# Two-layer spectral and squared-ReLU kernel: x loaded in pairs ahead of the constants, first-stage matrices scaled on POOL and ACT, mirrored filter rows placed by transfers, a new order table

## The chip, the cores and the metric

The kernel runs on one core of one Trainium2 chip. A core has five engines that run side by side and meet at semaphores: TensorE (PE, matmuls; its weight loads are shown as PEld), VectorE (DVE), ScalarE (ACT), GpSimd (POOL) and SyncE (SP, which here only issues transfers). Sixteen DMA engines move the data; SP, ACT and POOL issue to them. The metric is device time in microseconds (us), the median of several runs. The profile is of one further execution, and its times are counted from the first instruction.

## The reference

`x` is 2048 tokens by 448 features in bf16. Two layers are applied, each of a spectral part A and a dense part B, with the same weights in both layers:

```
def _A_ref(x, w_r, w_i):
    X = rfft2(x.astype(float32))
    X = X * (w_r + 1j * w_i)
    return irfft2(X, s=(S, D)).astype(bfloat16)

def _B_ref(x, w1, b1, w2, b2):
    h = einsum("bsd,df->bsf", x, w1) + b1
    h = relu(h) ** 2
    return einsum("bsf,fd->bsd", h, w2) + b2

x = x + _A_ref(_layernorm(x), A_w_r, A_w_i)
x = x + _B_ref(_layernorm(x), B_w1, B_b1, B_w2, B_b2)
x = x + _A_ref(_layernorm(x), A_w_r, A_w_i)
x = x + _B_ref(_layernorm(x), B_w1, B_b1, B_w2, B_b2)
```

The filter `w_r`, `w_i` has 2048 rows of 225 columns. The dense part goes from 448 to 1792 features and back.

## The kernel before

The tokens lie as 128 partitions by 16 tiles; a tile `t` is `[128, 448]`. Both Fourier transforms are written as matmuls with constant matrices. The work of layer 0 up to its dense part runs in these stages:

- **A1**, for each tile: mean and variance (`ln_stats`, on DVE with `bn_stats` and `bn_aggr`, or for tiles 1, 4 and 6 on ACT in two passes over the tile), the square root on ACT, the reciprocal `rstd` on DVE, and `m`, minus twice the mean (`minus`, L805). `first_A` then scales the 128x256 matrix `FA_sb` by `rstd` into a buffer `Fs` (L673) and lets PE multiply the tile by it: four products of 256 columns and one with `m`. The result is moved from the accumulators (`ps`) to `XA`. There are four buffers `Fs`, used in turn: the scaling for tile t waits until PE is done with tile t-4.
- **TD** and **B**, for each of eight frequency pairs: products with `TD_sb` (out to `U`) and with `G_sb` (out to `EF`); `U` and `EF` are parts of the buffer `arena`.
- **W**, the product with the filter, all on DVE: chains of `tensor_tensor` (L688) on `EF` and the filter rows in `Wt`. For a frequency pair, four rows are read: two as they lie in DRAM and two in mirrored order. The first chain, W0.0, reads the first frequency pair of `Wt`; the last, W0.7, ends the stage.
- **Bi**, **TI**, **AI**: the way back, products with `H_sb`, `HS_sb`, `TI_sb`, `FI_sb`; PE can do a part of Bi only when W has written its input. The stage ends in `x_sb`. The dense part follows, with `W1_sb` and `W2_sb`, then the same again for layer 1.

The mirrored filter rows come in three steps. POOL issues two gathers (L704) that read the rows of `w_i` and of `w_r` backwards into `Wm`, which lies in the buffer `yT`. When they have landed, POOL copies 14 pieces of 128x224 from there to `Wt` (L744 through the helper line L662). The other constants are loaded by plain transfers that SP issues, all of them after tile 4 of x has landed (`x4`, L747).

What sets the order: every operation is recorded once, and a scheduler (`schedule`) sorts the recorded units by the numbers in the table `ORDER`; a letter behind a number gives the engine (`p` POOL, `a` ACT, `d` DVE). While it walks the sorted list it keeps a model of the times of each engine. By this model it picks one of the eight accumulator banks for each result, and puts warming matmuls (on a matrix of ones, L1307) before a PE unit where the model says PE would wait. Each engine then runs its own instructions strictly in this order. The waits between engines are derived from which bytes are read and written.

Of the kernel before, what the change touches and what calls it, by code (L numbers as in the profile page):

```python
# [1384 lines left out]
```

## Time and profile before

| | us |
|---|---|
| median of 3 runs | 269.33 |
| lowest and highest run | 268.26 and 269.40 |
| span of the profiled execution, first to last instruction | 267.8 |

The time of the profiled execution as a whole is not given apart; the three runs lie 0.5 to 1.6 us above its span. In the page, "busy" is the time in which an engine had an instruction running. The rows of a timeline give the start and the length of a group of like instructions, then engine, line, operation, output and inputs, their shape and number, and in brackets how long the engine sat idle before them and what ended that. The rows that the prediction reads are quoted there.

### The profile page before, as it was taken

Reading aid. Unit: us, or ns where it says so; the run is one execution under the profiler, and the core shown is the slowest. Engines: PE = TensorE matmul, PEld = TensorE weight load, DVE = VectorE, ACT = ScalarE, POOL = GpSimd, SP = SyncE. Lnnn points to the kernel's source line nnn. Section 1 sums busy time; section 2 is a strip of 40 time slices with the busy share of each in tenths; the row PEclk is TensorE's granted clock in tenths of the full one; section 3 lists DMA queues with packets and bytes.
Section 4 is the critical chain, followed back from the end, with each engine's and each line's share of the span. In section 5 each row is a group of like instructions: output and inputs, shape, how many; then the busy total and the mean of one; then the engine's idle time right before and its main releaser. Section 6 shows DMA issues by size and latency. Waiting matters only on the chain. (4 is left out here: it accounts for less than half of the span.)

```text
span 267.8 us, 5840 instructions
## 1 busy us (share of the span) xinstructions
PE 259.3 (97%) x2194; PEld 158.9 (59%) x2194; DVE 212.7 (79%) x652; ACT 171.3 (64%) x391; POOL 14.4 (5%) x42
## 2 busy tenths in 40 slices
PE   6899999899999999999999999989999999999996
PEld 1477665798544544555559774779654554454554
DVE  5866999899996964999999899899998963463722
ACT  4688994979429755985128896889735753678000
POOL 0577000000000000000000000000000000000000
PEclk9999999999999999999999999999999999999999
DMA  6999370020420222300000000011232026200211
GB/s 222 305 376 354 74 228 17 0 42 10 54 52 2 39 43 44 68 0 0 2 0 4 2 2 0 2 23 22 39 73 42 0 42 111 89 2 0 70 39 47
DMA packets 27312, 17.03 MB, mean 64 GB/s; under 512 B 20210, under 2 KB 25810, under 8 KB 27156
## 3 DMA queue, kind: packets, MB, share of 16 engines
q1 hardware_dynamic: 26692, 14.82, 21.7%
q10 hardware_dynamic: 432, 1.03, 1.1%
q0 software_dynamic: 160, 0.81, 0.8%
q8 instruction: 17, 0.28, 0.5%
q14 instruction: 11, 0.09, 0.1%
HBM read 11.15 MB, written 1.84 MB: 48 GB/s over the span
## 5 line engine op out<-in xcount | busy, mean ns | idle before, releaser
L636 PE MATMUL ps<-yT,W_sb 64*128 64x512 bf16 (+1 forms) x770 | 90.3, 346 | 0.0
L636 PE MATMUL ps<-W_sb,arena 128*128 128x448 bf16 (+2 forms) x490 | 87.5, 336 | 0.0
L636 PEld LDWEIGHTS ps<-yT,W_sb 64*128 64x128 bf16 (+1 forms) x770 | 51.5, 95 | 36.0 <-issue 1.5
L636 PEld LDWEIGHTS ps<-W_sb,arena 128*128 128x128 bf16 x490 | 46.3, 98 | 36.3 <-DVE arena L688 0.8
L655 ACT ACTIVATE arena<-ps,b1col 128x512 bf16<-128x512 f32 x84 | 51.9, 691 | 14.2 <-PE ps L636 14.0
L688 DVE TENSOR_TENSOR arena<-arena 128x512 bf16<-128x512 bf16 (+1 forms) x140 | 45.7, 367 | 18.0 <-ACT arena L655 17.6
L1109 ACT ACTIVATE VT<-x_sb 128x448 bf16<-128x448 bf16 x32 | 18.4, 577 | 13.4 <-DVE x_sb L1085 13.3
L661 ACT ACTIVATE arena<-ps 128x448 bf16<-128x448 f32 (+1 forms) x44 | 25.1, 693 | 2.4 <-PE ps L636 2.2
L1205 DVE SCALAR_TENSOR_TENSOR x_sb<-ps,arena 128x448 bf16<-128x448 f32 (+2 forms) x27 | 15.2, 570 | 14.1 <-PE ps L636 13.7
L655 ACT ACTIVATE mv<-mv,epst 128x1 f32<-128x1 f32 (+1 forms) x46 | 12.6, 294 | 17.2 <-DVE mv L794 12.1
L655 ACT ACTIVATE arena<-ps 128x256 bf16<-128x256 f32 x56 | 17.8, 392 | 4.0 <-PE ps L636 3.7
L661 ACT ACTIVATE XA<-ps 128x512 bf16<-128x512 f32 x29 | 15.6, 592 | 3.2 <-PE ps L636 3.2
L661 ACT ACTIVATE VT<-ps 128x512 bf16<-128x512 f32 (+1 forms) x26 | 13.0, 567 | 7.0 <-PE ps L636 6.9
L636 PE MATMUL ps<-yT,VT 64*128 64x512 bf16 x42 | 15.8, 376 | 0.0
L636 PE MATMUL ps<-HS_sb,arena 128*128 128x512 bf16 x64 | 14.9, 380 | 0.1
L636 PE MATMUL ps<-arena,G_sb 128*128 128x448 bf16 (+1 forms) x76 | 14.4, 333 | 0.5 <-ACT arena L661 0.4
L672 ACT ACTIVATE arena<-x_sb,rstd 128x448 bf16<-128x448 bf16 x11 | 7.2, 666 | 10.5 <-DVE rstd L1124 6.0
L636 PE MATMUL ps<-TD_sb,XA 112*64 112x112 bf16 (+2 forms) x312 | 13.2, 224 | 0.0
L636 PE MATMUL ps<-Fs,xin 128*128 128x256 bf16 x64 | 10.0, 290 | 3.0 <-DVE mv L784 2.9
L636 PEld LDWEIGHTS ps<-TD_sb,XA 112*64 112x64 bf16 (+2 forms) x312 | 12.1, 108 | 1.1 <-issue 0.6
L688 DVE TENSOR_TENSOR tmp<-arena,Wt 128x896 bf16<-128x896 bf16 (+1 forms) x14 | 11.4, 852 | 1.7 <-ACT arena L661 1.5
L1135 DVE SCALAR_TENSOR_TENSOR arena<-x_sb,mv,b2row 128x448 bf16<-128x448 bf16 x16 | 10.7, 679 | 0.1
(76 smaller groups left out, 300.9 us busy)
## 6 DMA issues: line engine op xcount, KB each, us to landing
out_dram<-x_sb SPq DMA_DIRECT2D x15, 112.0 KB, 1.7
W_sb<-in_B_w_dram SPq DMA_DIRECT2D x1, 1568.0 KB, 16.1
W_sb<-in_B_w_dram SPq DMA_DIRECT2D x1, 1344.0 KB, 6.7
HS_sb<-c_HS SPq DMA_DIRECT2D x1, 1024.0 KB, 11.2
G_sb<-c_G SPq DMA_DIRECT2D x1, 960.0 KB
...
Wt<-in_A_w_i_dram SPq DMA_DIRECT2D x1, 392.0 KB, 4.7
```

Of the source, the lines that this page charges most:

```text
L636: return sch.add("pe", lambda e: e.matmul(_res(o), lhsT, rhs, start=start, stop=stop, skip_group_check=skip), [lhsT, rhs], [o], cost=cost, ...
L655: sch.add("act", lambda e: e.activation(o, _res(i), func, **kw), rd, [o], cost=c)
L661: op = sch.add(engs[0], lambda e: e.activation(o, _res(i), ACT.Copy) if h[0].eng == "act" else e.tensor_copy(o, _res(i)), [i], [o], cost=c ...
L672: op = sch.add(engs[0], lambda e: e.activation(o, i, ACT.Copy, scale=s) if h[0].eng == "act" else e.tensor_scalar(o, i, s, 1.0, op0=ALU.mu ...
L688: sch.add(eng, lambda e: e.tensor_tensor(o, _res(a), b, op), [a, b], [o], cost=_free(o) / rate + 69.0)
L1109: sch.add("act", lambda e, i=i, o=o, x=x: e.activation(o, x, ACT.Square, accum_out=mv[:, i, 4:5]), [x], [o, mv[:, i, 4:5]], cost=560.0)
L1135: small(lambda e, o=o, x=x, m=m: e.scalar_tensor_tensor(out=o, in0=x, scalar=m, in1=b2row[:], op0=ALU.add, op1=ALU.add), [x, m, b2row[:]], ...
L1205: small(lambda e: e.scalar_tensor_tensor(out=o, in0=_res(i), scalar=r[0] if r else 1.0, in1=xb[:, t, d0:d1], op0=ALU.mult, op1=ALU.add), [ ...
```

## The change

It has six parts, all in the first stages of layer 0 and in the order table.

1. **x in pairs.** The 16 tiles came in seven transfers of one or four tiles; they now come as tile 0, tile 1 and then pairs. SP issues tile 0 and six pairs, ahead of all constants; ACT issues tile 1, `FA_sb` (before: SP's third transfer) and tiles 4 and 5. The constants now wait for tile 7 and no longer for tile 4.
2. **Scaling on POOL and ACT.** The scaled matrix of each tile is written to the tile's own place in `x_sb`, which is free at that time, and not to one of four buffers. 15 of the 16 scalings are on POOL and one on ACT; before, 10 were on POOL and 6 on DVE. The clearing of `x_sb`'s spare columns moves behind A1.
3. **Mirrored rows by transfers.** The 14 copies on POOL are replaced by two transfers from `Wm` to `Wt` that SP issues; they run backwards over seven rows of 224. The two gathers are moved to the front of POOL's work and wait for tile 0 only.
4. **Unbroken dummies.** The warming matmuls are no longer put in by the scheduler's model; a table `WARM` gives 15 of them in one run before the first product of A1.
5. **Banks in the table.** The bank of each result now stands in `ORDER` behind a colon; the model of times in `schedule` is gone. The walk through the sorted list adds the waits for a bank's last readers as before.
6. **A new `ORDER`.** Units of A1, TD, B, W, Bi, TI and AI of layer 0 and of the first part of its dense stage stand in another order. From the middle of that dense part on, the order is the old one with numbers lower by ten.

```diff
-    "dve.warm": "1", "dve.epst": "4", "sp.xin": "0 12 15 18", "act.xin": "11 14 17", "sp.FA_sb": "13",
+    "dve.warm": "2", "dve.epst": "3", "sp.xin": "4 8 11 12 13 14 15", "act.xin": "6 9", "act.FA_sb": "7",
...
-    "A1.0": "6 7 24 26 9p 28d 64 99a", "A1.1": "23 25 30 32 39 27d 70p 71 111a", "A1.2": "20 21 29 34 22p 67p 68 78a",
+    "A1.0": "5 26 29 30 32d 31p 53:0 60a", "A1.1": "27 34 36 37 41 28p 42p 66:1 88a", "A1.2": "33 39 46 47 40p 52p 68:2 135d",
...
+WARM = {53: ((7, 512), (7, 512), (7, 512), (7, 512), (7, 512), (7, 512), (7, 512), (7, 512), (7, 512), (7, 512), (7,
+    512), (7, 512), (7, 512), (7, 256), (7, 128))}
...
     def schedule(self):
...
+        for n, u in enumerate(self.ranked()):
+            for b, w in WARM.get(n, ()):
+                d = _Op("pe", self.warm_fn(b, w), False, 0.0, 0.0)
+                take(b, d)
...
-        for n, (a, b, e) in enumerate(((0, 1, "sp"), (1, 2, "act"), (2, 3, "sp"), (4, 8, "act"), (3, 4, "sp"), (8, 12, "act"),
-                                       (12, 16, "sp"))):
+        for n, (a, b, e) in enumerate(((0, 1, "sp"), (1, 2, "act"), (2, 4, "sp"), (4, 6, "act"), (6, 8, "sp"), (8, 10, "sp"),
+                                       (10, 12, "sp"), (12, 14, "sp"), (14, 16, "sp"))):
             dma(e, xin[:, a:b, :], x_dram[:, a:b, :])
-            if n == 2:
-                dma("sp", FA_sb[:], dc["FA"])
+            if n == 1:
+                dma("act", FA_sb[:], dc["FA"])
...
-            gather(Wm[:, i, :], w.rearrange("s (l o) -> (s l) o", o=1), back[:, 0:1], xin[:, 4, :])
-        for p in range(7):
-            for i in range(2):
-                sch.tag = f"M.{p}"
-                evac(Wp[:, p, 3 - 2 * i, :], Wm[:, i, :].rearrange("p (k l) -> p k l", k=7)[:, 6 - p, 1:225], ["pool"])
-        sch.tag = ""
+            gather(Wm[:, i, :], w.rearrange("s (l o) -> (s l) o", o=1), back[:, 0:1], xin[:, 0, :])
+        for i in range(2):
+            dma("sp", Wp[:, :, 3 - 2 * i, :], Wm[:, i, :].rearrange("p (k l) -> p k l", k=7)[:, ::-1, 1:225])
         memset(Z[:, :, LW:256], 0.0)
-        x4 = [xin[:, 4, :]]
+        x4 = [xin[:, 7, :]]
...
-                x, f = xin[:, t, :], Fs[:, t % NFS, :]
+                x, f = xin[:, t, :], x_sb[:, t, 0:2 * P]
                 scaled(f, FA_sb[:], r, EV["FS"])
```

**POOL, from its first memset of the kernel on.** `m` is minus twice a tile's mean, `Fs` (now `x_sb`) the scaled matrix, the two rows named DMA are the gathers. Before:

```order
L709 MEMSET ones 128x128
L805 ISA
L805 TENSOR_SCALAR m<-mv 128x1
L735 IOTA back 128x1
L805 TENSOR_SCALAR m<-mv 128x1
L704 DMA yT<-in_A_w_i_dram,back 128x1575
L805 TENSOR_SCALAR m<-mv 128x1
L673 TENSOR_SCALAR Fs<-FA_sb,rstd 128x256 x3
```

Now:

```order
L629 MEMSET ones 128x128
L653 ISA
L653 IOTA back 128x1
L624 DMA yT<-in_A_w_i_dram,back 128x1575
L624 DMA yT<-in_A_w_r_dram,back 128x1575
L720 TENSOR_SCALAR m<-mv 128x1
L593 TENSOR_SCALAR x_sb<-FA_sb,rstd 128x256
```

Both gathers now stand ahead of the first scaling; the second one stood behind the sixth scaling on POOL before.

**SP, its first transfers.** `Wt<-yT` are the mirrored rows, `Wt<-in_A_w` the rows as they lie. Before:

```order
L628 DMA xin<-in_A_x_dram 128x448 x2
L628 DMA FA_sb<-c_FA 128x256
L628 DMA xin<-in_A_x_dram 128x448
L628 DMA xin<-in_A_x_dram 128x1792
L628 DMA G_sb<-c_G 128x768
L628 DMA Wt<-in_A_w_i_dram 128x2x224
L628 DMA Wt<-in_A_w_i_dram 128x7x224
L628 DMA TD_sb<-c_TD 128x896
L628 DMA G_sb<-c_G 128x3840
L628 DMA Wt<-in_A_w_r_dram 128x7x224
L628 DMA HS_sb<-c_HS 128x4096
```

Now:

```order
L548 DMA xin<-in_A_x_dram 128x448
L548 DMA xin<-in_A_x_dram 128x896 x6
L548 DMA Wt<-in_A_w_r_dram 128x2x224
L548 DMA Wt<-in_A_w_i_dram 128x2x224
L548 DMA Wt<-in_A_w_i_dram 128x7x224
L548 DMA H_sb<-c_H 128x1024
L548 DMA TD_sb<-c_TD 128x896
L548 DMA Wt<-in_A_w_r_dram 128x7x224
L548 DMA G_sb<-c_G 128x768
L548 DMA G_sb<-c_G 128x3840
L548 DMA Wt<-yT 128x7x224 x2
```

All of x and the plain filter rows moved ahead of the large constant `G_sb`; the mirrored rows stand right behind it, with three others between them and `HS_sb`.

More of the change, by code (lines that the diff above doesn't have):

```diff
@@ L126 @@
 ORDER = {
[33 rows of a table removed]
[32 rows of a table added]
     "h0.0.0": (
[2 rows of a table removed]
[2 rows of a table added]
     "h0.0.2": (
[48 rows of a table removed]
[49 rows of a table added]
     "h1.0.0": (
[2 rows of a table removed]
[3 rows of a table added]
     "h1.0.2": (
[4 rows of a table removed]
[4 rows of a table added]
     "h1.1.0": (
[3 rows of a table removed]
[3 rows of a table added]
     "h1.2.0": (
[3 rows of a table removed]
[3 rows of a table added]
     "h1.3.0": (
[4 rows of a table removed]
-}
-EV = {'A1': ['act', 'dve'], 'A2': ['act'], 'TD': ['act', 'dve'], 'B': ['act', 'dve'], 'Bi': ['act', 'dve'], 'Bi0': ['act', 'dve'], 'TI': ['act', 'dve'], 'M': ['act', 'dve'], 'T': ['act', 'dve'], 'XR': ['pool'], 'FS': ['pool', 'dve'], 'XN1': ['dve'], 'FS2': ['dve'], 'XN': ['act', 'dve']}
[4 rows of a table added]
+}
+WARM = {53: ((7, 512), (7, 512), (7, 512), (7, 512), (7, 512), (7, 512), (7, 512), (7, 512), (7, 512), (7, 512), (7,
+    512), (7, 512), (7, 512), (7, 256), (7, 128))}
+EV = {'A1': ['act', 'dve'], 'A2': ['act'], 'TD': ['act', 'dve'], 'B': ['act', 'dve'], 'Bi': ['act', 'dve'], 'Bi0': ['act', 'dve'], 'TI': ['act', 'dve'], 'M': ['act', 'dve'], 'T': ['act', 'dve'], 'XR': ['pool'], 'FS': ['pool', 'act'], 'XN1': ['dve'], 'FS2': ['dve'], 'XN': ['act', 'dve']}
 SPLIT = (1, 2, 4)
@@ L327 @@
     DMA_RATE = 350.0
-    TURN = (200.0, 100.0)
-    SLACK = 60.0
-    DMA_SLACK = 200.0
-    BEGIN = 800.0
-    WINDOW = 3413.0
     def __init__(self):
@@ L342, in __init__ @@
         self.lead = {}
-        self.warm_from = 0.0
-        self.cold_until = 0.0
-        self.warm_share = 0.7
     def add(self, eng, fn, reads=(), writes=(), is_dma=False, cost=100.0, lat=130.0, unit=None):
@@ L403, in ranked @@
             if u.tag in ORDER:
-                w = ORDER[u.tag].split()[k]
+                w = ORDER[u.tag].split()[k].split(":")
+                for t, b in zip(u.tiles, w[1] if len(w) > 1 else ""):
+                    t.bank = int(b)
+                w = w[0]
                 if w[-1].isalpha():
@@ L415, in schedule, with take @@
     def schedule(self):
-        free = dict.fromkeys(self.ENGINES, self.BEGIN)
-        free["pe"] = self.warm_from
-        bank_free = [0.0] * NB
-        bank_user = [None] * NB
-        dma_free = 0.0
-        rows = 128
-        used = []
-        done = {}
-        def ready(op):
-            r = 0.0
-            for d in op.gdeps:
-                if d.unit is op.unit or (d.eng == "pe" and op.eng == "pe"):
-                    continue
-                if d.is_dma:
-                    r = max(r, done[d] + 130.0 + self.DMA_SLACK)
-                else:
-                    r = max(r, done[d] + d.lat + (80.0 if op.eng == "pe" else 0.0) + (self.SLACK if d.eng != op.eng else 0.0))
-            return r
-        def pick(n, now, taken):
-            best = None
-            for b in range(0, NB, n):
-                if any(i in taken for i in range(b, b + n)):
-                    continue
-                if all(bank_user[i] is None or all(op in done for op in bank_user[i].readers) for i in range(b, b + n)):
-                    f = max(bank_free[b:b + n])
-                    key = (max(f, now), n == 1 and bank_free[b ^ 1] <= now, f)
-                    if best is None or key < best[0]:
-                        best = (key, b)
-            assert best is not None, "no bank is free"
-            return best[1]
-        for u in self.ranked():
-            e = u.eng
-            first = free[e] + (self.TURN[u.rows < 128] if e == "pe" and u.rows != rows else 0.0)
-            taken = []
-            for w in u.tiles:
-                now = max(first, ready(u.ops[0])) + sum(op.cost for op in u.ops[:u.ops.index(w.first)])
-                w.bank = pick(w.n, now, taken)
-                taken += range(w.bank, w.bank + w.n)
+        user = [None] * NB
+        def take(b, op):
+            if user[b] is not None:
+                op.deps.extend(r for r in user[b].readers if r not in op.deps)
+        for n, u in enumerate(self.ranked()):
+            for b, w in WARM.get(n, ()):
+                d = _Op("pe", self.warm_fn(b, w), False, 0.0, 0.0)
+                take(b, d)
+                if not self.ops["pe"]:
+                    d.deps.extend(self.warm_deps)
+                self.ops["pe"].append(d)
             for op in u.ops:
-                t = max(first if op is u.ops[0] else free[e], ready(op))
                 for w in u.tiles:
@@ L461, in schedule @@
                         for i in range(w.bank, w.bank + w.n):
-                            old = bank_user[i]
-                            if old is not None:
-                                t = max(t, bank_free[i] + 80.0 + self.SLACK)
-                                for rd in old.readers:
-                                    if rd not in op.deps:
-                                        op.deps.append(rd)
-                            bank_user[i] = w
-                if e == "pe" and op is u.ops[0]:
-                    while t - free["pe"] >= 120.0:
-                        f = free["pe"]
-                        cold = f < self.cold_until
-                        recent = sum(min(b, t) - max(a, t - self.WINDOW) for a, b in used[-90:] if b > t - self.WINDOW)
-                        if not (cold or recent < self.warm_share * self.WINDOW):
-                            break
-                        n = next((n for n in (512, 256, 128) if (n / 2.4 + 2.5) * (2.0 if cold else 1.0) + 60.0 <= t - f), 0)
-                        if not n:
-                            break
-                        b = min(((bank_free[b], b) for b in range(NB) if b not in taken and (
-                            bank_user[b] is None or all(x in done for x in bank_user[b].readers))), default=None)
-                        if b is None:
-                            break
-                        if b[0] > f:
-                            free["pe"] = b[0]
-                            continue
-                        c = (n / 2.4 + 2.5) * (2.0 if cold else 1.0)
-                        d = _Op("pe", self.warm_fn(b[1], n), False, c, 195.0)
-                        if bank_user[b[1]] is not None:
-                            d.deps.extend(bank_user[b[1]].readers)
-                        if not self.ops["pe"]:
-                            d.deps.extend(self.warm_deps)
-                        self.ops["pe"].append(d)
-                        used.append((f, f + c))
-                        free["pe"] = f + c
-                    t = max(t, free["pe"])
-                    begin = t
@@ L497, in schedule @@
-                t += op.cost
-                free[e] = t
-                done[op] = t
-                self.ops[e].append(op)
-                if op.is_dma:
-                    done[op] = dma_free = max(dma_free, t + 1800.0) + op.lat
-                    if e == "pool":
-                        done[op] = max(dma_free, t + 7000.0)
-                for w in op.takes:
-                    for i in range(w.bank, w.bank + w.n):
-                        bank_free[i] = max(bank_free[i], t + op.lat)
@@ L508, in schedule @@
-            if e == "pe":
-                rows = u.rows
-                used.append((begin, free["pe"]))
-        self.length = max(done.values())
-        self.used = used
-        self.done = done
+                            take(i, op)
+                            user[i] = w
+                self.ops[u.eng].append(op)
         for e in self.ENGINES:
@@ L629, in dma @@
                 sch.add(eng, fn, reads, writes, is_dma=True, cost=450.0,
-                        lat=2.0 * n / sch.DMA_RATE)
+                        lat=2.0 * n / sch.DMA_RATE + (n * 0.8 if list(i.ap)[-1][0] != 1 else 0.0))
         def mm(o, lhsT, rhs, start, stop, skip=False, unit=None):
@@ L701, in gather @@
             n = 1
-            for step, cnt in list(i.ap):
+            for step, cnt in list(o.ap):
                 n *= cnt
@@ L722, in bass_interleave_layers__spectral_gfnet__dense_activation_squared_relu__prompt_kernel @@
         memset(epst[:, 0:1], EPS)
-        for n, (a, b, e) in enumerate(((0, 1, "sp"), (1, 2, "act"), (2, 3, "sp"), (4, 8, "act"), (3, 4, "sp"), (8, 12, "act"),
-                                       (12, 16, "sp"))):
+        for n, (a, b, e) in enumerate(((0, 1, "sp"), (1, 2, "act"), (2, 4, "sp"), (4, 6, "act"), (6, 8, "sp"), (8, 10, "sp"),
+                                       (10, 12, "sp"), (12, 14, "sp"), (14, 16, "sp"))):
             dma(e, xin[:, a:b, :], x_dram[:, a:b, :])
-            if n == 2:
-                dma("sp", FA_sb[:], dc["FA"])
+            if n == 1:
+                dma("act", FA_sb[:], dc["FA"])
             if n == 3:
                 sch.add("act", lambda e: e.activation(warm[:, 0:1], warm[:, 0:1], ACT.Sqrt), [warm[:, 0:1]], [warm[:, 0:1]],
-                        cost=200.0)
+                        cost=1480.0)
         memset(ones[:], 1.0, eng="pool")
         sch.warm_deps = sch.lead["pool"] = [sch.last_write[k] for k in _pages(ones[:])][:1]
-        sch.warm_from = 1000.0
-        sch.cold_until = 4800.0
         sch.add("pool", lambda e: e.iota(back[:, 0:1], pattern=[[0, 1]], base=(16 * (P - 1) + 9) * 225, channel_multiplier=-16 * 225), [],
```

190 rows, old and new, of the table ORDER are left out of this document.

## Prediction

> **What bounds the kernel now.** I read first the page's busy shares, then the stretches of 5 us, then the timelines of PE, DVE and POOL up to 46 us, and last the transfers.
>
> ```profile
> PE 259.3 (97%) x2194; PEld 158.9 (59%) x2194; DVE 212.7 (79%) x652; ACT 171.3 (64%) x391; POOL 14.4 (5%) x42
> ...
> 0.00:5.00 5.00, 4.02 (x9) 1.19 (x9) 2.65 (x7) 2.96 (x7) 0.67 (x7) 1.00 0.61 177
> 5.00:10.00 5.00, 2.05 (x9) 1.19 (x9) 3.39 (x15) 2.44 (x10) 2.53 (x5) 1.00 0.97 319
> 10.00:15.00 5.00, 5.00 (x30) 3.13 (x28) 3.83 (x20) 2.50 (x11) 2.13 (x6) 1.00 1.03 338
> 45.00:50.00 5.00, 4.99 (x52) 3.98 (x51) 3.43 (x7) 4.34 (x9) 0.00 (x0) 1.00 0.00 0
> 65.00:70.00 5.00, 5.00 (x34) 3.12 (x32) 4.80 (x20) 3.54 (x13) 0.00 (x0) 1.00 0.58 57
> ```
>
> A stretch lists busy time of PE, PEld, DVE, ACT and POOL, the granted clock, the share of the DMA engines and GB/s. PE is busy throughout, except at the start: 5 to 10 us has 2.05 us of it. From 45 us on PE has no room, so a microsecond gained before that should last to the end. What PE does early shows only in its timeline:
>
> ```profile
> 0.98 4.02 PE L1307 MATMUL ps<-ones 128*128 128x512 bf16 x9 [0.98 <-POOL ones L709]
> 7.95 1.01 PE L636 MATMUL ps<-Fs,xin 128*128 128x256 bf16 x4 [2.95 <-DVE mv L784]
> 8.97 3.19 PE L1307 MATMUL ps<-ones 128*128 128x512 bf16 x7
> 11.96 1.06 PE L636 MATMUL ps<-Fs,xin 128*128 128x256 bf16 x4
> 13.02 0.60 PE L636 MATMUL ps<-Fs,xin 128*128 128x256 bf16 x4
> 13.57 0.60 PE L636 MATMUL ps<-Fs,xin 128*128 128x256 bf16 x4
> ...
> 21.15 2.46 PE L636 MATMUL ps<-TD_sb,XA 128*128 128x224 bf16 x24
> 37.89 6.67 PE L636 MATMUL ps<-HS_sb,arena 128*128 128x512 bf16 x28
> 44.40 1.04 PE L636 MATMUL ps<-H_sb,arena 128*128 128x256 bf16 x8
> ```
>
> Nine dummies, nothing for 2.95 us, tile 0, then seven more dummies in the way until 11.96. Only from 13.02 on does a tile take 0.55 us (13.02 to 13.57); the four products before took 1.01 to 1.06 us, those after 0.60, though the granted clock reads 1.00. A1 ends at 21.15. Next, DVE:
>
> ```profile
> 3.31 0.63 DVE L793 BATCH_NORM_STATS2 st<-xin 128x6 f32<-128x448 bf16 x1 [0.28 <-DMA xin<-in_A_x_dram]
> 7.52 0.28 DVE L673 TENSOR_SCALAR Fs<-FA_sb,rstd 128x256 bf16<-128x256 bf16 x1 [0.73 <-DMA FA_sb<-c_FA]
> ...
> 25.21 1.61 DVE L688 TENSOR_TENSOR tmp<-arena,Wt 128x896 bf16<-128x896 bf16 x2 [1.55 <-ACT arena L661]
> 28.26 1.16 DVE L688 TENSOR_TENSOR tmp<-arena 128x896 bf16<-128x896 bf16 x2
> 43.71 0.39 DVE L688 TENSOR_TENSOR arena<-tmp 128x448 bf16<-128x448 bf16 x1
> ```
>
> The filter stage W runs on DVE from 25.21 to 44.10 almost without a gap, and the last product that needs it starts at 44.40. So two chains matter: PE from the start of TD (21.15), and DVE from the start of W (25.21). The later one sets the gain.
>
> **Start of A1.** Tile 0 was ready to be scaled when `FA_sb` landed, at 7.5 (row 7.52). Now `FA_sb` is second on ACT. Tile 1, first on ACT, was issued at 0.72 and landed 2.8 us later.
>
> ```profile
> 0.72 0.90 ACTq L628 DMA_DIRECT2D xin<-in_A_x_dram  x2
> xin<-in_A_x_dram ACTq DMA_DIRECT2D x1, 112.0 KB, 2.8
> 7.62 1.23 POOL L704 DMA_INDIRECT yT<-in_A_w_i_dram,back  x1 [0.65 <-POOL m L805]
> 15.57 1.03 POOL L704 DMA_INDIRECT yT<-in_A_w_r_dram,back  x1 [0.15 <-issue]
> 17.12 0.20 POOL L805 TENSOR_SCALAR m<-mv 128x2 bf16<-128x2 f32 x1
> 17.30 0.48 POOL L673 TENSOR_SCALAR Fs<-FA_sb,rstd 128x256 bf16<-128x256 bf16 x1
> 17.97 0.94 POOL L673 TENSOR_SCALAR Fs<-FA_sb,rstd 128x256 bf16<-128x256 bf16 x2
> ```
>
> Behind tile 1 (3.5) the 64 KB and what SP sends meanwhile (at most a pair, 224 KB) are under 1 us at 319 GB/s: about 4.4, and no later than the 7.5 of before. But the gathers now stand ahead of POOL's first scaling. They begin when tile 0 has landed (3.3) and take 1.23 + 1.03, with 0 to 0.65 us ahead of the first (its row's idle time): POOL is free at 5.6 to 6.2. I take 6.0; with one `m` (0.18) and one scaling (0.48) PE can start at 6.7. The 15 dummies, at 0.447 each (4.02 / 9) and less for the two short ones, end near 7.1 at the slow pace: both meet, and PE loses at most some tenths.
>
> **Length of A1.** POOL then has 15 scalings at 0.47 (0.94 for two) and 11 `m` at 0.18 (17.12 to 17.30): 7.05 + 1.98 = 9.0 us, from 6.0 to 15.0. The waits for PE go with the buffers. DVE loses its six scalings; per tile it needs 0.63 to 0.86 us:
>
> ```profile
> 10.15 0.59 DVE L793 BATCH_NORM_STATS2 st<-xin 128x6 f32<-128x448 bf16 x1
> 10.78 0.60 DVE L793 BATCH_NORM_STATS2 st<-xin 128x6 f32<-128x448 bf16 x1
> 11.64 0.59 DVE L793 BATCH_NORM_STATS2 st<-xin 128x6 f32<-128x448 bf16 x1
> ```
>
> Twelve tiles more from about 4.7 end at 12.3 to 15.0, so POOL, not DVE, is the bound, though DVE could reach it. PE's 16 tiles at 0.55 from 7.1 end at 15.9. After POOL's last scaling PE needs 0.6 more: 15.6. I take **TD at 15.9**, 5.25 us earlier (bounds 15.4 and 17.5, the second if DVE or the square roots on ACT, each queued behind evacuations, add their 2 us). From TD to W it took 25.21 - 21.15 = 4.06, and the evacuations on ACT may trail by 0.5: by the engines, W could start at 20.0 to 20.5.
>
> **Transfers.** W0.0 also needs the mirrored rows. These were copied on POOL from 22.09 on, beside other work. Now they are two transfers behind everything in SP's queue up to `G_sb`. In bytes of the shapes: x 1.84 MB, `FA_sb` 0.07, gathers 0.81, plain filter rows 0.23 + 0.80, part of `H_sb` 0.26, `TD_sb` 0.23, `G_sb` 0.20 + 0.98; together 5.4 MB, and 0.80 MB of mirrored rows.
>
> ```profile
> 2.00:18.00 16.00, 13.00 (x68) 7.29 (x66) 10.78 (x45) 10.53 (x32) 7.68 (x21) 1.00 1.01 327
> 8.00:10.00 2.00, 2.00 (x8) 1.11 (x9) 2.00 (x9) 1.51 (x6) 1.96 (x4) 1.00 0.99 249
> 18.00:20.00 2.00, 2.00 (x20) 1.64 (x17) 1.55 (x7) 1.75 (x5) 1.38 (x4) 1.00 0.99 376
> 22.09 4.96 POOL L662 COPY Wt<-yT 128x224 bf16<-128x224 bf16 x13 [2.71 <-DMA yT<-in_A_w_r_dram,back]
> yT<-in_A_w_r_dram,back POOLq DMA_INDIRECT x1, 6.5
> 6.39 1.31 SPq L628 DMA_DIRECT2D Wt<-in_A_w_i_dram  x2
> Wt<-in_A_w_i_dram SPq DMA_DIRECT2D x1, 392.0 KB, 4.7
> ```
>
> The engines are full from 2 to 18 us (share 1.01) at 327 GB/s, with the same mix of rows: 5.4 MB are through at 2 + 16.5 = 18.5. `G_sb` is thus there just as the first B wants it (15.9 + 2.3). The gathers, issued by 5.8, land by 12.3 at 6.5 us each; SP holds there until then, which costs nothing while the engines have a backlog. The mirrored rows are 448 bytes long, SBUF to SBUF, which no plain transfer here shows. Nearest are the plain filter rows of the same length, issued from 6.39 to 7.70 and landed 4.7 us after their issue, so mostly moving at 8 to 10 us: 249 GB/s, so 3.2 us. At 376 it is 2.1. I take 327, 2.5 us, and some tenths until the semaphore: **W starts at 21.2**, 4.0 us earlier; bounds 20.5 and 22.2. The transfer, not the engines, is then last.
>
> The Trainium skill, "DMA: Bandwidth & Descriptors", Specifications, says that rows under 512 bytes fall below line rate, through a read-modify-write. The row 8 to 10 agrees in direction, 249 against 376; the page has no figure for 448, and by its direction W would start at about 21.9.
>
> **W and after.** The first two W operations took 1.61 us beside POOL's copies, like ones 1.16 (row 28.26): without the copies 0.45 less. The rest, 17.3 us, stays. W ends at 21.2 + 18.9 - 0.45 = 39.65 and not at 44.10: **4.45 us**. PE's own work from TD to 44.40 is 23.25 us long at most, from 15.9 to 39.15, so DVE still decides. From there on the shift should be carried along. The new order of TI and of the first dense products may save or add what PE waits there:
>
> ```profile
> 52.09 0.27 PE L636 MATMUL ps<-J_sb,x_sb 128*128 128x128 bf16 x2 [0.64 <-DVE x_sb L688]
> ```
>
> 0.64 either way; I take 0. The later constants stand behind fewer bytes than there is time; I cost them at nothing, as the engines are nearly idle from 40 us on. The moved memset (0.48) and the bank table add no work on the bound.
>
> Sum: span 267.8 - 4.45 = 263.35. The runs' median lies 1.5 above the span; with the same, **264.9**.
>
> **The rivals.**
>
> *The mirrored rows are later than I think*: the rows at 249 GB/s or slower, SP held up at `G_sb`, the gathers late. W at 23 to 24 gives a gain of 1.65 to 2.65: 266.7 to 267.7. For it speaks that DMA is full to the end; against it, that the 448-byte rows of before were read in the same mix. Chance 0.17.
>
> *PE starts A1 slow.* The rows show a slow pace until 13.0, five microseconds after 7.95, and 4.02 us of dummies alone did not end it. If the unbroken dummies end in the same pace, tiles take some 1.1 us until it lifts; 3 us of that cost about 1.5 in A1, TD starts at 17.4, W at 21.9: 265.6. Chance 0.10. The Trainium skill, "TensorE: Matmul & The Clock Gate", Part 1, has a window of 3.4 us that runs freely and must be busy throughout; by it, an estimate, the pace may lift anywhere from 4.4 to 7.8 here. The rows agree (7.95 to 13.0 holds one such window).
>
> *The gain is lost later*: the first dense products meet late weights, or the new order around TI makes PE wait. 267 to 268.5. Against it, the transfer-free stretch at 45 to 50. Chance 0.08.
>
> *Slower*: SBUF-to-SBUF rows are dear. The one such traffic in the trace, the transposes, moved 57 GB/s at a share of 0.58 (row 65 to 70), so 98 GB/s when full. At that price 0.80 MB takes 8.2 us, W starts at 27.1, and the time is 267.8 + 1.9 - 0.45 + 1.5 = 270.8. It turns slower once the rows land after 25.7, below 110 GB/s. Against it: those pieces are far shorter (256 bytes), and transposed. Chance 0.08.
>
> **How the numbers follow.** Forecast 0.57, with 263.0 (W by the engines at 20.0, TI's 0.64 saved: 6.3 us gained) to 266.2. The range must take in most of the first rival and part of the third: 263.0 to 267.7. About 0.5%, 1.35 us, is what a measurement can tell from no change, so faster means below 268.0. Faster: 0.57 + 0.17 + 0.10 of the first cases less a few hundredths, with a third of the third: 0.83; slower 0.07; same 0.10.
>
> **What would show it.** First product of A1 near 7; tiles at 0.55 to 0.6; POOL without waits from 6 to 15; TD near 15.9; the first `tmp<-arena,Wt` on DVE at 21.2 released by the transfer `Wt<-yT`, not by ACT; its pair at 1.2; W's end at 39.7; the stretches from 45 us on equal, shifted. The forecast is wrong if W starts after 23, if PE stands still in TI or the first dense part, or if a tile still takes over 1 us after 9 us.

## The result, and the profile after

| | before | after |
|---|---|---|
| median, us | 268.51 (5 runs) | 266.56 (5 runs) |
| lowest and highest | 268.26 and 269.40 | 266.28 and 267.40 |
| span of the profiled execution | 267.8 | 264.6 |

The ratio is 0.9923, with an interval of 0.9901 to 0.9945. The changed kernel is 2.0 us faster by these runs and 3.2 us faster by the two profiled executions. Beside a later set of runs it was 0.9935 (0.9906 to 0.9965): 266.49 against 268.01. Over all 88 undisturbed runs of this study, the kernel before has a median of 268.0 and goes from 266.2 to 269.8. So its profiled execution, a span of 267.8 and about 1.8 outside it, was one of its latest, and 1.5 us is the better figure for the gain.

The timeline of PE in the changed kernel, start and length in us, then the group:

```profile
0.98 5.24 PE L1222 MATMUL ps<-ones 128*128 128x512 bf16 x15 [0.98 <-POOL ones L629]
7.44 0.60 PE L556 MATMUL ps<-x_sb,xin 128*128 128x256 bf16 x4 [1.23 <-POOL x_sb L593]
...
8.99 0.60 PE L556 MATMUL ps<-x_sb,xin 128*128 128x256 bf16 x4 [0.85 <-POOL x_sb L593]
...
9.65 0.60 PE L556 MATMUL ps<-x_sb,xin 128*128 128x256 bf16 x4
...
10.96 0.60 PE L556 MATMUL ps<-x_sb,xin 128*128 128x256 bf16 x4
...
17.80 2.46 PE L556 MATMUL ps<-TD_sb,XA 128*128 128x224 bf16 x24
...
40.76 1.04 PE L556 MATMUL ps<-H_sb,arena 128*128 128x256 bf16 x8
...
42.80 1.41 PE L556 MATMUL ps<-TI_sb,VT 112*128 112x224 bf16 x13
```

The dummies end at 6.2, and after 1.23 us the first tile runs at the fast pace (0.60 for four products, where before had 1.01). Yet the first tile is at 7.44, the second waits until 8.99, the fifth (tile 8) starts at 10.96, and TD at 17.80 (before 21.15). The last product that needs W is at 40.76 (44.40), TI at 42.80. ACT's timeline in the changed kernel shows why the second tile is late:

```profile
7.22 0.58 ACT L696 ACTIVATE yT<-xin 128x448 bf16<-128x448 bf16 x1 [2.16 <-DMA xin<-in_A_x_dram]
...
7.80 0.46 ACT L575 ACTIVATE mv<-mv,epst 128x1 f32<-128x1 f32 x2
```

POOL's timeline has the end of the gathers and the first scaling:

```profile
5.66 0.95 POOL L624 DMA_INDIRECT yT<-in_A_w_r_dram,back  x1 [0.31 <-DVE mv L699]
...
6.81 0.49 POOL L593 TENSOR_SCALAR x_sb<-FA_sb,rstd 128x256 bf16<-128x256 bf16 x1
```

And DVE's has the reciprocal that tile 1 waits for, and the first two groups of W:

```profile
8.11 0.16 DVE L715 RECIPROCAL rstd<-mv 128x1 f32<-128x1 f32 x1 [2.08 <-ACT mv L575]
...
21.94 1.16 DVE L608 TENSOR_TENSOR tmp<-arena,Wt 128x896 bf16<-128x896 bf16 x2 [0.99 <-DMA Wt<-yT]
...
24.73 1.16 DVE L608 TENSOR_TENSOR tmp<-arena 128x896 bf16<-128x896 bf16 x2 [0.17 <-ACT arena L581]
```

ACT's pass over tile 4 waits 2.16 us for its transfer, until 7.22. The square roots of tiles 1 and 2 stand behind it (7.80), and DVE's reciprocal behind those (8.11). At 21.94 W starts when the mirrored rows have landed, as forecast; the row at 24.73, however, is released by ACT. The stretches (columns as in the prediction):

```profile
5.00:10.00 5.00, 2.93 (x20) 1.59 (x19) 2.92 (x13) 2.72 (x12) 3.62 (x9) 1.00 1.04 378
10.00:15.00 5.00, 4.87 (x44) 3.67 (x42) 5.00 (x23) 4.91 (x16) 4.72 (x16) 1.00 1.15 336
45.00:50.00 5.00, 4.72 (x63) 3.75 (x62) 4.99 (x12) 5.00 (x14) 0.00 (x0) 1.00 0.01 3
```

PE has 2.93 us of work between 5 and 10 us, against 2.05 before, and in 45 to 50 it still has little room (4.72 of 5).

### The profile page after: what moved, and what is told of

Same layout as the page of the kernel before. It is cut to its first block, busy times and chain, and to the rows that moved or that the text cites. A ratio compares the mean times of both kernels' runs of the same rounds, so it can differ in the third digit from the quotient of the medians.

```text
span 264.6 us, 5791 instructions
## 1 busy us (share of the span) xinstructions
PE 257.3 (97%) x2191; PEld 161.4 (61%) x2193; DVE 210.9 (80%) x645; ACT 171.9 (65%) x392; POOL 11.5 (4%) x34
## 5 line engine op out<-in xcount | busy, mean ns | idle before, releaser
L556 PEld LDWEIGHTS ps<-yT,W_sb 64*128 64x128 bf16 (+1 forms) x770 | 54.6, 95 | 32.4 <-issue 1.5
L608 DVE TENSOR_TENSOR arena<-arena 128x512 bf16<-128x512 bf16 (+1 forms) x140 | 44.9, 368 | 17.9 <-ACT arena L575 17.5
L581 ACT ACTIVATE XA<-ps 128x512 bf16<-128x512 f32 x28 | 15.0, 590 | 1.0 <-PE ps L556 1.0
L592 ACT ACTIVATE arena<-x_sb,rstd 128x448 bf16<-128x448 bf16 x12 | 7.8, 669 | 10.7 <-DVE rstd L1039 6.0
L556 PE MATMUL ps<-x_sb,xin 128*128 128x256 bf16 x64 | 9.1, 272 | 2.2 <-POOL x_sb L593 2.1
```

The lines of the kernel that those rows point to most:

```text
L556: return sch.add("pe", lambda e: e.matmul(_res(o), lhsT, rhs, start=start, stop=stop, skip_group_check=skip), [lhsT, rhs], [o], cost=cost, ...
L581: op = sch.add(engs[0], lambda e: e.activation(o, _res(i), ACT.Copy) if h[0].eng == "act" else e.tensor_copy(o, _res(i)), [i], [o], cost=c ...
L592: op = sch.add(engs[0], lambda e: e.activation(o, i, ACT.Copy, scale=s) if h[0].eng == "act" else e.tensor_scalar(o, i, s, 1.0, op0=ALU.mu ...
L608: sch.add(eng, lambda e: e.tensor_tensor(o, _res(a), b, op), [a, b], [o], cost=_free(o) / rate + 69.0)
```

## The experiments

All numbers of profiles come first; each kernel's edit, expectation and reading follow. "First" is the first product of A1, "W" the first `tmp<-arena,Wt` on DVE; the times are starts in us in the profiled execution, the median is that of the runs.

| kernel | first | TD | W | W - TD | TI - TD | span | span - TD | median (runs) |
|---|---|---|---|---|---|---|---|---|
| before | 7.95 | 21.15 | 25.21 | 4.06 | 24.99 | 267.8 | 246.65 | 268.0 (88) |
| `c0_before` | 6.78 | 19.18 | 23.24 | 4.06 | 25.18 | 266.0 | 246.82 | 267.94 (12) |
| `b_dum` | 7.30 | 18.80 | 22.86 | 4.06 | 25.84 | 266.3 | 247.50 | 267.43 (12) |
| after | 7.44 | 17.80 | 21.94 | 4.14 | 25.00 | 264.6 | 246.80 | 266.56 (5) |
| `c1_after` | 7.39 | 17.91 | 22.27 | 4.36 | 24.99 | 264.8 | 246.89 | 266.49 (7) |
| `u_copies` | 7.47 | 17.87 | 21.70 | 3.83 | 24.99 | 264.6 | 246.73 | 266.66 (12) |
| `u_dum9` | 7.43 | 19.57 | 23.41 | 3.84 | 24.99 | 266.4 | 246.83 | 267.45 (12) |
| `e_rows` | 7.52 | 17.34 | 21.17 | 3.83 | 24.99 | 264.0 | 246.66 | 265.77 (6) |
| `e_act` | 7.53 | 16.65 | 21.33 | 4.68 | 25.27 | 263.8 | 247.15 | 265.71 (7) |
| `e_both` | 7.46 | 17.02 | 20.85 | 3.83 | 24.99 | 263.7 | 246.68 | 265.31 (6) |
| `v_dve` | 5.61 | 17.55 | 21.38 | 3.83 | 24.99 | 264.4 | 246.85 | 265.94 (9) |
| `f_stats` | 7.46 | 17.23 | 21.07 | 3.84 | 24.99 | 263.9 | 246.67 | 265.70 (6) |
| `f_all` | 6.16 | 17.22 | 21.05 | 3.83 | 24.99 | 264.1 | 246.88 | 265.91 (6) |
| `f_xsp` | 7.43 | 16.51 | 22.80 | 6.29 | 27.99 | 266.2 | 249.69 | 265.26 (7) |

**The kernel before once more** (`c0_before`, no edit).

> The kernel before, unchanged, to see several spans of it. The profiled execution had a span of 267.8, the runs shown fell near 268.3 and near 269.4. If the profiled execution is one of the later kind, spans of about 266.6 and of about 267.7 both occur, and the difference arises within the span, before 13 us, where PE still runs at its slow pace. Rival: all spans are near 267.8 and the scatter lies outside the span; then the start of A1 is the same in each profile.

The spans of the runs went from 264.7 to 267.6 with no two clusters, and a second profile of the same program had its TD 1.97 us earlier than the first. Its PE timeline:

```profile
0.98 3.52 PE L1307 MATMUL ps<-ones 128*128 128x512 bf16 x9 [0.98 <-POOL ones L709]
6.78 0.60 PE L636 MATMUL ps<-Fs,xin 128*128 128x256 bf16 x4 [2.28 <-DVE mv L784]
...
7.36 3.19 PE L1307 MATMUL ps<-ones 128*128 128x512 bf16 x7
10.35 0.77 PE L636 MATMUL ps<-Fs,xin 128*128 128x256 bf16 x4
```

The scaling of tile 0 on DVE, which stood at 7.52 in the other profile:

```profile
6.34 0.29 DVE L673 TENSOR_SCALAR Fs<-FA_sb,rstd 128x256 bf16<-128x256 bf16 x1
```

Three of its stretches, with the columns as above:

```profile
6.00:8.00 2.00, 1.22 (x7) 0.82 (x8) 1.74 (x8) 1.60 (x6) 1.07 (x2) 0.82 1.00 382
8.00:10.00 2.00, 2.00 (x6) 0.68 (x5) 2.00 (x13) 1.57 (x7) 1.96 (x6) 0.50 0.96 250
10.00:12.00 2.00, 2.00 (x16) 1.52 (x15) 2.00 (x9) 1.48 (x5) 0.53 (x3) 0.83 0.98 330
```

Here PE became fast within the first nine dummies (3.52 us, where the other profile had 4.02), did tile 0 in 0.60, and then fell back: the column behind POOL, the granted clock, is 0.50 in 8 to 10 us. In the profile of the prediction it never became fast before 13.0. The scatter of the kernel before is thus within its span and in A1, and these two profiles show two parts of it. Of the 1.97 us, 1.17 are there at the first product already (6.78 and 7.95), as `FA_sb` landed at 5.94 and not at 7.49; the other 0.80 come from when the pace lifts and falls around PE's idle time of 2 to 3 us.

**Both limits of the changed kernel, one at a time and together** (`e_rows`, `e_act`, `e_both`).

`e_rows`:

```diff
-    "sp.Wt": "65 63 25 22 20 21", "dve.arena": "0", "sp.J_sb": "194", "sp.TD_sb": "24", "sp.G_sb": "62 50",
-    "sp.H_sb": "69 23", "sp.HS_sb": "150", "sp.TI_sb": "224", "sp.FI_sb": "141", "sp.b2row": "167", "sp.b1in": "155",
+    "sp.Wt": "65 63 25 22 150 150", "dve.arena": "0", "sp.J_sb": "194", "sp.TD_sb": "24", "sp.G_sb": "62 50",
+    "sp.H_sb": "69 150", "sp.HS_sb": "150", "sp.TI_sb": "224", "sp.FI_sb": "141", "sp.b2row": "167", "sp.b1in": "155",
```

`e_act`; `e_both` has both:

```diff
-    "A1.3": "38 43 51 55 44p 61p 70:3 117a", "A1.4": "35 48 87 89 97 73p 103a 104:7 140a",
+    "A1.3": "38 43 51 55 44p 61p 70:3 117a", "A1.4": "51 51 87 89 97 73p 103a 104:7 140a",
```

(In `WARM` the place of the dummies is counted in units; it goes from 53 to 50 where three units leave the front, and to 48 where five do, so that they stay where they were.)

> The changed kernel with three transfers (two of the plain rows 0 and 8 of the filter, 0.23 MB, and the first part of H_sb, 0.26 MB) moved from ahead of TD_sb to behind HS_sb, so that 0.49 MB less stand ahead of the mirrored rows. If the landing of the mirrored rows sets the start of W: they land 1.4 earlier, near 20.4, W starts at 20.95 (DVE is free then) in place of 21.94, and the time falls by 0.7 to 1.0, to about 265.7. If A1 and PE's own work from TD on set the time: W starts earlier, PE's waits in the H and HS products shrink, and what is gained is lost again before TI; within 0.3 of 266.5. If mixed rows slow each other, the mirrored rows land less than 0.5 earlier.

> The changed kernel with ACT's two passes over tile 4, which wait for a transfer that landed at 7.2, moved behind the square roots of tiles 1, 2 and 3. If those passes held up A1: the second tile's first product, 8.99 before, starts near 7.9, TD near 16.5 in place of 17.8. If the mirrored rows then set W, W stays at 21.8 to 21.9 and the time within 0.3 of 266.5; if A1 and PE set the time, it falls by about 1 to 265.5. If the late landing of tiles 4 to 7 itself is the limit, TD stays within 0.3 of 17.8.

> Both edits. If the two limits stand one behind the other, the sum is more than the parts: mirrored rows at 20.4, engines ready near 19.7, W at 20.5, H products 1.4 earlier than 40.76, time about 265.1. If only the transfer matters, the same as the rows alone (265.7); if only A1, the same as the passes alone.

DVE's start of W in `e_act`:

```profile
21.33 1.16 DVE L608 TENSOR_TENSOR tmp<-arena,Wt 128x896 bf16<-128x896 bf16 x2 [1.54 <-ACT arena L581]
```

And in `e_both`, with the second group:

```profile
20.85 1.38 DVE L608 TENSOR_TENSOR tmp<-arena,Wt 128x896 bf16<-128x896 bf16 x2 [0.69 <-ACT arena L581]
...
23.95 1.16 DVE L608 TENSOR_TENSOR tmp<-arena 128x896 bf16<-128x896 bf16 x2 [0.26 <-ACT arena L581]
```

In `e_rows` the mirrored rows landed at 20.86 and W no longer waited for them: it started at TD + 3.83, released by ACT. But relative to TD nothing moved; TI came at TD + 24.99 as in the changed kernel. The 0.7 to 0.8 us in the median cannot come from W. TD itself was 0.46 earlier there, as tiles 4 to 7 landed at 6.6 to 6.7 and not at 7.0 to 7.2, which the edit does not touch; why they did is open. `e_act` did what its first theory says in A1: the second tile at 8.13 in place of 8.99, no wait above 0.2 for the tiles behind it, TD at 16.65. Not all of this is the edit's, since x also came earlier there, which the edit does not touch: tiles 4 to 7 landed at 5.80 to 6.40 and not at 6.95 to 7.20, tiles 8 and 9 at 6.55 and not at 7.58. `e_rows` and `e_both` differ by this edit alone, and x landed alike in both (tiles 8 and 9 at 7.19 and 7.11): between them TD moves by 0.32 and the median by 0.46 (six runs each). `e_act` also shows W held by the transfer: the rows landed at 21.21, W started 0.12 later, at TD + 4.68 (the row names ACT, which was due at TD + 3.83). W was 0.85 late by this and TI only 0.28. With both edits TD is at 17.02, W is free, and the median is 265.31, with no run above 265.82; the changed kernel had 265.76 to 267.40. Against the kernel before the ratio is 0.9909 (0.9882 to 0.9937). The runs of the changed kernel were made in other sets, so that this version, with a few numbers of the order table moved, is faster than the kernel before, and probably than the changed kernel too: all its runs lie below eleven of the twelve of that one.

**What sets the end from TD on** (`c1_after`, no edit; `u_copies`). In `u_copies` POOL copies the mirrored rows again, behind its last scaling:

```diff
-        for i in range(2):
-            dma("sp", Wp[:, :, 3 - 2 * i, :], Wm[:, i, :].rearrange("p (k l) -> p k l", k=7)[:, ::-1, 1:225])
+        for p in range(7):
+            for i in range(2):
+                sch.tag = f"M.{p}"
+                evac(Wp[:, p, 3 - 2 * i, :], Wm[:, i, :].rearrange("p (k l) -> p k l", k=7)[:, 6 - p, 1:225], ["pool"])
```

> The changed kernel, unchanged, beside the others of this call. In the six profiles so far the span ends 246.6 to 247.2 after TD's first product, whatever W does. If the start of TD sets the end, this profile too has a span of its TD start plus 246.7 within 0.2, and its runs scatter less than those of before (3.5), as its A1 has no product at the slow pace. If W sets the end, the span follows W's start instead (21.94 gave 264.6).

> The changed kernel with the mirrored rows copied by POOL again (14 copies behind its last scaling, which ended near 15) in place of the two SBUF transfers. If W's start by the transfer set the time, as the prediction had it, W starts at TD + 3.8 without the wait (about 0.3 to 0.9 earlier), but its first pairs are slower beside the copies (0.45 before): between 0.5 faster and 0.3 slower than the changed kernel. If the start of TD sets the end, the time is the same within 0.3 although the transfers are gone: the third part of the change is worth nothing by itself.

The start of TD sets the end, as long as W is not late by more than it can spare. The two kernels start W 0.57 us apart (22.27 and 21.70) and have the same TD, the same TI (42.90 and 42.86) and the same time within 0.2. DVE in `u_copies`:

```profile
21.70 1.38 DVE L608 TENSOR_TENSOR tmp<-arena,Wt 128x896 bf16<-128x896 bf16 x2 [0.69 <-ACT arena L581]
...
24.80 1.16 DVE L608 TENSOR_TENSOR tmp<-arena 128x896 bf16<-128x896 bf16 x2 [0.26 <-ACT arena L581]
```

DVE in `c1_after`:

```profile
22.27 1.16 DVE L608 TENSOR_TENSOR tmp<-arena,Wt 128x896 bf16<-128x896 bf16 x2 [1.22 <-DMA Wt<-yT]
```

Where W starts early, its first pair takes 1.38 for 1.16, since the second operation starts 0.76 and not 0.54 behind the first, and DVE waits 0.26 for ACT at 24.80, which is TD + 6.93; so it does in `e_both` (23.95, also TD + 6.93). This second group of W, not the first, paces the rest, and it hangs on PE's products from TD on by way of ACT. W's first group has some 0.55 us of slack against it.

**The dummies** (`u_dum9`: nine of 512 columns in place of the 15 in `WARM`; `b_dum`: the kernel before with seven more behind its ninth).

```diff
+                        if len(self.ops["pe"]) == 9:
+                            for _ in range(7):
+                                self.ops["pe"].append(_Op("pe", self.warm_fn(b[1], n), False, c, 195.0))
```

> The changed kernel with 9 dummies in place of 15, so that PE stands still from about 4.9 to 7.4 as it did before. If unbroken work is what lifts the pace before A1, the first tiles run at 1.0 to 1.1 each until about 11 to 13, TD starts 1.5 to 2.5 later than with 15, and the runs scatter as those of before did: about 268.3. If 9 dummies are enough, TD stays at 17.8 and the time at 266.5.

> The kernel before with 7 dummies more behind its first nine, so that PE's work before tile 0 is unbroken until about 6 to 7; nothing else changed. If the broken dummies were the largest part of what the change removes (with 9 in place of 15 the changed kernel lost 0.96 in the median), tile 0 and the seven dummies behind it run at the fast pace, the second tile starts at 9.3 to 10 instead of 10.35 to 11.96, TD near 18.5 to 19.0, the median falls by 0.7 to 1.2 from 267.9 to about 267.0, and the runs scatter by less than 1.5 in place of 3. If the late landing of FA_sb and the scaling on DVE set A1 before, the second tile waits for POOL or DVE until 10.3 anyway and the median stays within 0.3 of 267.9.

PE in `u_dum9`:

```profile
0.98 4.02 PE L1221 MATMUL ps<-ones 128*128 128x512 bf16 x9 [0.98 <-POOL ones L628]
7.43 1.01 PE L555 MATMUL ps<-x_sb,xin 128*128 128x256 bf16 x4 [2.44 <-POOL x_sb L592]
...
12.60 1.03 PE L555 MATMUL ps<-x_sb,xin 128*128 128x256 bf16 x4
...
13.57 0.60 PE L555 MATMUL ps<-x_sb,xin 128*128 128x256 bf16 x4
...
19.57 2.46 PE L555 MATMUL ps<-TD_sb,XA 128*128 128x224 bf16 x24
```

PE in `b_dum`:

```profile
0.98 5.03 PE L1310 MATMUL ps<-ones 128*128 128x512 bf16 x16 [0.98 <-POOL ones L712]
7.30 0.60 PE L639 MATMUL ps<-Fs,xin 128*128 128x256 bf16 x4 [1.29 <-DVE mv L787]
...
7.84 1.67 PE L1310 MATMUL ps<-ones 128*128 128x512 bf16 x7
9.35 0.60 PE L639 MATMUL ps<-Fs,xin 128*128 128x256 bf16 x4
...
18.80 2.46 PE L639 MATMUL ps<-TD_sb,XA 128*128 128x224 bf16 x24
```

POOL in `b_dum`, behind A1:

```profile
16.66 0.37 POOL L665 COPY Wt<-yT 128x224 bf16<-128x224 bf16 x1
21.97 8.14 POOL L665 COPY Wt<-yT 128x224 bf16<-128x224 bf16 x13 [4.94 <-DMA yT<-in_A_w_r_dram,back]
```

Six dummies fewer, and the first five tiles run at 1.01 to 1.06; the fast pace comes at 13.57, TD 1.66 later than in `c1_after`. The median is 0.96 higher (267.45, where 268.3 was expected), and the runs go from 266.2 to 269.0, like those of before. From the other side, seven dummies more make the kernel before faster by 0.6 (267.43 against 268.0 over all its runs), or by 0.9 going by the ratio to the runs beside it (0.9965, 0.9945 to 0.9984), and its runs go from 266.5 to 268.1. The forecast of 267.0 was not reached. Its profile, taken in its slowest run, shows a new limit that may be why: the second gather, behind six scalings, lands at 21.92, and the copies wait for it until 21.97 and take 8.14 us beside W. TI - TD is 25.84 there.

The mean granted clock of each run bears this out. One stretch of 3.4 us at 0.50, as in `c0_before`'s profile, makes it 0.994 there. Of the 83 later runs of the kernel before 33 have 0.994, of the twelve of `u_dum9` seven have 0.994 or 0.987, of the twelve of `b_dum` none, and of the 71 runs with 15 dummies four have 0.993 or 0.994, each the slowest of its kernel (267.40 for the changed one). So unbroken dummies make the fall rare and do not exclude it. A pace that lifts late does not show in this figure: the profile of the prediction reads 1.00 until 13.0.

**Further edits on top of `e_both`** (`v_dve`: tiles 0 and 1 scaled on DVE; `f_xsp`: tiles 4 and 5 issued by SP; `f_stats`: DVE's statistics of tiles 8 and 9 behind the reciprocals of tiles 2 and 3; `f_all`: all three).

`v_dve` (with DVE among the engines of `FS`):

```diff
-    "dve.b1col": "465", "sp.W1_sb": "145 226 239 261", "sp.W2_sb": "177", "A1.0": "5 26 29 30 32d 31p 53:0 60a",
-    "A1.1": "27 34 36 37 41 28p 42p 66:1 88a", "A1.2": "33 39 46 47 40p 52p 68:2 135d",
+    "dve.b1col": "465", "sp.W1_sb": "145 226 239 261", "sp.W2_sb": "177", "A1.0": "5 26 29 30 32d 31d 53:0 60a",
+    "A1.1": "27 34 36 37 41 42d 42d 66:1 88a", "A1.2": "33 39 46 47 40p 52p 68:2 135d",
```

`f_xsp`:

```diff
-    "dve.warm": "2", "dve.epst": "3", "sp.xin": "4 8 11 12 13 14 15", "act.xin": "6 9", "act.FA_sb": "7",
+    "dve.warm": "2", "dve.epst": "3", "sp.xin": "4 8 9 11 12 13 14 15", "act.xin": "6", "act.FA_sb": "7",
...
-        for n, (a, b, e) in enumerate(((0, 1, "sp"), (1, 2, "act"), (2, 4, "sp"), (4, 6, "act"), (6, 8, "sp"), (8, 10, "sp"),
+        for n, (a, b, e) in enumerate(((0, 1, "sp"), (1, 2, "act"), (2, 4, "sp"), (4, 6, "sp"), (6, 8, "sp"), (8, 10, "sp"),
```

`f_stats`:

```diff
-    "A1.7": "105 109 111 114 110p 115p 118:3 142a", "A1.8": "49 57 45 56 58 67 75p 74p 76:0 94a 77p 78:4 130a",
+    "A1.7": "105 109 111 114 110p 115p 118:3 142a", "A1.8": "55 57 55 56 58 67 75p 74p 76:0 94a 77p 78:4 130a",
```

> Both edits of the call before (three transfers behind HS_sb, ACT's passes over tile 4 behind the square roots), and the scaled FA_sb of tiles 0 and 1 made on DVE, so that PE doesn't wait for POOL's gathers to end at 6.6. If the start of A1's products sets TD, and TD the end: first product where the dummies end (5.7 to 6.9) in place of 7.5, TD near 15.9 to 16.3, mirrored rows at 19.6 in time for W, time 264.5. If the landing of tiles 4 to 7 (6.2 to 7.2) or POOL's rate binds, PE waits at the third to fifth tile and the time stays at 265.3.

> Both edits (three transfers behind HS_sb, ACT's passes over tile 4 behind the square roots), and tiles 4 and 5 issued by SP in place of ACT, so that between 3.75 and 5.75 one queue runs and not two. With two queues some 36 packets of 1792 bytes went in 0.25 us there, later with one 50 to 56. If sharing by two queues slows them, tiles 4 to 7 land about 1 earlier (5.5 to 6.2) and the median falls by 0.3 to 0.8 from 265.31, to about 264.8; if not, they land within 0.3 of 6.2 to 6.9 and the time stays.

> Both edits, and DVE's statistics of tiles 8 and 9, which wait for a transfer that lands at 6.6 to 7.7, moved behind the reciprocals of tiles 2 and 3. If they hold up those tiles as ACT's passes did, the products of the third and fourth tile never wait for POOL, and the start of TD depends less on the transfers; median 0 to 0.4 below 265.31. If POOL is the limit there, no change.

> All edits together: the three transfers, ACT's passes, DVE's statistics of tiles 8 and 9, tiles 4 and 5 on SP, tiles 0 and 1 scaled on DVE. If the start of TD sets the end and only these stood before it: first product at 5.6 to 6.2, no wait of over 0.3 until the fifth tile, TD at 16.2 to 16.6 and, with span = TD + 246.7 and 1.8 outside the span, 264.7 to 265.1 in time. If the transfers of tiles 4 to 9 bind, PE waits at the fifth tile for POOL until about 10 and TD stays near 16.9: 265.4.

PE's first tiles in `f_all`:

```profile
6.16 0.60 PE L556 MATMUL ps<-x_sb,xin 128*128 128x256 bf16 x4
...
6.98 0.60 PE L556 MATMUL ps<-x_sb,xin 128*128 128x256 bf16 x4
...
7.81 0.60 PE L556 MATMUL ps<-x_sb,xin 128*128 128x256 bf16 x4
...
8.35 0.60 PE L556 MATMUL ps<-x_sb,xin 128*128 128x256 bf16 x4
...
10.34 0.60 PE L556 MATMUL ps<-x_sb,xin 128*128 128x256 bf16 x4 [1.29 <-POOL x_sb L593]
```

And the fifth tile in `v_dve`, whose first is at 5.61:

```profile
10.68 0.60 PE L556 MATMUL ps<-x_sb,xin 128*128 128x256 bf16 x4 [0.27 <-POOL x_sb L593]
```

None is measurably better than `e_both`. With the first four tiles ready by 8.35, PE stands until 10.34 for the fifth: it needs a transfer that lands near 7, then DVE's statistics, a square root, a reciprocal and POOL. An earlier first product only makes this wait longer; TD is at 17.2 and the median at 265.91. The fifth tile is the one that counts in all ten profiles with 15 dummies: TD starts 6.7 to 6.9 after it, wherever the four before it stand. `f_xsp`'s median is that of `e_both`, so the second queue was not what held tiles 4 to 7 up, as far as the times tell; tile 4 was there by 6.43 in its profile, but with two queues it was at 6.40 in `e_act`. Its profile was taken in its slowest run (268.0; the six others are at 265.1 to 265.7), and that run shows the price of a late W. DVE:

```profile
22.80 1.16 DVE L608 TENSOR_TENSOR tmp<-arena,Wt 128x896 bf16<-128x896 bf16 x2 [3.15 <-DMA Wt<-yT]
```

PE in the same profile, in the products of Bi:

```profile
32.23 3.61 PE L556 MATMUL ps<-H_sb,arena 128*128 128x256 bf16 x20 [1.64 <-DVE arena L608]
...
36.48 6.14 PE L556 MATMUL ps<-HS_sb,arena 128*128 128x512 bf16 x26 [0.22 <-issue]
```

Three stretches of it, where the granted clock is the number behind POOL's:

```profile
32.00:34.00 2.00, 1.63 (x13) 1.20 (x14) 2.00 (x4) 0.37 (x1) 0.00 (x0) 0.95 0.92 157
34.00:36.00 2.00, 2.00 (x10) 1.25 (x9) 2.00 (x5) 1.03 (x2) 0.00 (x0) 0.50 1.02 328
36.00:38.00 2.00, 1.78 (x7) 0.81 (x7) 1.90 (x3) 0.00 (x0) 0.00 (x0) 0.70 1.11 346
```

Here TD was the earliest of all (16.51), but the second transfer of the mirrored rows landed only at 22.68, and W was 2.46 late. PE stood 1.64 us for W, after which its clock was granted at 0.50 from about 34 on; TI came 3.00 late.

## Why the prediction came out as it did

The time was forecast at 264.9, in a range of 263.0 to 267.7; it is 266.56. Faster was right, but the gain is less than half of the 4.4 us that the sum has, and the time lies close to what the first rival (mirrored rows that land late, 266.7 to 267.7) would have given, without that rival's mechanism. That the range holds it is owed to its width. Step by step:

- **Start of A1.** `FA_sb` landed at 4.46 (forecast 4.4), POOL was free at 6.6 (6.0): the first gather began at 4.21, 0.9 after tile 0 had landed, and the second only at 5.66. The first product came at 7.44 (7.1). In the profile the dummies left no slow pace behind them: right, and the rival "PE starts A1 slow" fell. `u_dum9` shows that it was a real danger.
- **Length of A1.** This is the mis-sized term: TD at 17.80 and not 15.9, beyond the bound of 17.5. Of the 1.9 us, 0.34 is the later start and about 1.6 are waits; a tile that does not wait takes 0.55, as forecast. "POOL without waits" failed: tiles 4 to 7 landed at 6.95 to 7.20, tiles 8 and 9 at 7.58, and ACT, which takes its instructions in order, held the square roots of tiles 1 and 2 behind a pass over tile 4. The pass is worth 0.3 in TD where x lands alike (`e_rows` against `e_both`); `e_act` gets 16.65, where x came earlier as well. By these rows the larger part goes with the landing of x. The prediction gave POOL its work from 6.0 on without asking when the tiles land, and named DVE and ACT's evacuations as what might delay A1, not a transfer or a pass that waits for one.
- **Transfers.** `G_sb` landed at 19.11 and not at 18.5, the mirrored rows at 20.35 and 21.82: 2.7 us for both, between the two bounds (2.1 and 3.2). W started at 21.94 (forecast 21.2), released by them. The rival with 98 GB/s fell: 0.80 MB in 2.7 us is 296 GB/s. The Trainium skill, "DMA: Bandwidth & Descriptors", Bandwidth, has that transfers from SBUF to SBUF don't suffer the penalty of small descriptors, which the prediction, going by its Specifications, did not take in. The landings, at no less than the 249 GB/s of the plain rows, speak for that, and the 21.94 met the 21.9 of the prediction's sentence by luck, as `G_sb` was late.
- **"The transfer, not the engines, is then last", and the gain follows W.** This step failed. The row at 21.94 is true, but the wait that it shows was worth nothing: W's second group waits for ACT at TD + 6.93 anyway, and TI - TD is 25.0 wherever W starts between 3.83 and 4.36 after TD. The sum had used W's start as the end of the chain and its 18.9 us as fixed; the 0.45 saved in its first pair is lost again at the second group. With `u_copies`, which lacks the third part of the change, the median is 0.17 higher and the span 0.2 shorter: the runs don't resolve any gain by that part, as long as the gathers are early.
- **From TI on.** Span less TI is 221.66 before and 221.80 after: carried along, as forecast. The gain that was seen at 40.76 (3.64) shrank to 3.34 at TI, where PE then waited 0.6 for ACT's evacuation.
- **The base.** The sum was made against one execution that was some 1.6 us later than the median of its own kernel (267.8 + 1.8 against 268.0; the 1.5 of the sum was taken across executions). The forecast gain of 4.4 was therefore too large by about as much, whatever the steps: with the TD of a usual run, 268.0 - 1.8 - 246.7 = 19.5, the changed kernel gains 1.6 to 1.7.

What the gain consists of: the unbroken dummies, 0.6 to 0.9 (alone on the kernel before) or 1.0 (taken out of the changed kernel) of 1.5; the rest is the earlier x and `FA_sb`, the early gathers and the order, which were not told apart; the transfers of mirrored rows, nothing that these runs resolve.

On the pace, the rows: 15 dummies took from 4.57 to 5.87 us in the ten profiles that have them. Of the three with nine, which took 3.52 or 4.02, two were slow at the first tile and the third fell back right behind it. The Trainium skill, "TensorE: Matmul & The Clock Gate", Part 1, has it that the pace doubles after a busy window of about 3.4 us which runs freely, so that the moment differs from run to run. The rows agree: the dummies start 0.43 apart at first and 0.22 apart later, and the 1.3 us between 4.57 and 5.87 fit a moment that differs. In `e_both`, at 5.87, the dummies start 0.43 apart to the last, so that 15 is hardly one too many.
